# Transposing by DMA in place of TensorE, and alternating weight-gradient passes with dx tiles

## The chip, the cores and the metric

The kernel runs on one core of a Trainium2 chip. The metric is the device time of one execution in microseconds (us). Engines are named as in the profile: PE is TensorE (PEld its weight loads), DVE is VectorE, ACT is ScalarE, POOL is GpSimd, SP is SyncE, which here only issues DMAs (transfers between memories that the DMA engines carry out). A queue name with a q (SPq, ACTq) is the sequencer that issues. To evict is to copy a finished result of PE out of its result memory (PSUM) by ACT or DVE. The granted clock is the share of full speed at which the profile shows PE running.

Executions of one kernel mostly agree within about 1%. The granted TensorE clock differs a little from run to run (0.92 to 0.97 in the runs below), and the time goes with it. A run more than 1.5% above the fastest of its kernel is told slow. Medians below are over all runs, ratios over the fast ones, and a difference under about 8 us is not explained from single traces.

## The reference, cut to what matters

The reference computes an output and, by `vjp`, seven results in all: the output, dx, and the gradients of five weights. S = 2048 tokens, D = 512, F = 1792, 32 heads of 16.

```python
def _fwd_reference(A_x, A_wqkv, A_wo, B_x, B_w_gate, B_w_up, B_w_down):
    xn = _layernorm(A_x)
    s = linear_attention(xn @ A_wqkv) @ A_wo      # phi(q), phi(k), v; kv and z summed over tokens
    g = _silu((_sigmoid(xn @ B_w_gate) * (xn @ B_w_up)) @ B_w_down)
    return A_x + s * g

def reference(...):
    _out, _vjp = jax.vjp(_f, A_x, A_wqkv, A_wo, B_w_gate, B_w_up, B_w_down)
    return (_out, *_vjp(grad_out))
```

What matters: the gradient of a weight sums over the tokens, and this kernel's matmuls sum over the partitions of their operands, so both operands need the tokens on the partitions. Stage 2 produces the gradients dg, du and the activation hh with features on the partitions. Somebody has to transpose 3 x 1792 x 2048 values, 22 MB in bf16.

Of the kernel before, what the change touches and what calls it, by code (L numbers as in the profile page):

```python
# [27 lines left out]
def kernel(  # L28
# [28 lines left out]
    xn_d = dram.tile([NST, P, D], bf16, name="xn_d")  # L57
    xnT_d = dram.tile([NST, P, KT * P], bf16, name="xnT_d")
    pq_d = dram.tile([NST, P, D], bf16, name="pq_d")
    pqT_d = dram.tile([NST, P, KT * P], bf16, name="pqT_d")  # L60
    pkT_d = dram.tile([NST, P, KT * P], bf16, name="pkT_d")
    vT_d = dram.tile([NST, P, KT * P], bf16, name="vT_d")
# [6 lines left out]
    hhT_d = dram.tile([NST, P, FT * P], bf16, name="hhT_d")  # L69
    dgT_d = dram.tile([NST, P, FT * P], bf16, name="dgT_d")  # L70
    duT_d = dram.tile([NST, P, FT * P], bf16, name="duT_d")
# [42 lines left out]

    with ExitStack() as p1ctx:
# [3 lines left out]
        nc.sync.dma_start(out=xall[:, 0:2, :], in_=x2[0:256, :].rearrange("(t p) d -> p t d", p=P))  # L119
        nc.sync.dma_start(out=Wqkv_sb, in_=A_wqkv.rearrange("(kt p) n -> p kt n", p=P))  # L120
        nc.sync.dma_start(out=xall[:, 2:NST, :], in_=x2[256:S, :].rearrange("(t p) d -> p t d", p=P))
# [6 lines left out]
        sp1 = p1ctx.enter_context(tc.tile_pool(name="sp1", bufs=5))  # L128
# [18 lines left out]
        def do_wt_jobs(n):  # L147
            for _ in range(n):
                if not wt_jobs:
                    return  # L150
                dst, blocks = wt_jobs.pop(0)
                nb = len(blocks)
                pW = ps1.tile([P, 8, P], bf16, name="pW", tag="wt", bufs=1)
                for k, blk in enumerate(blocks):
                    nc.tensor.transpose(pW[:, k, :], blk, ident)
                if wt_flip[0] % 2 == 0:
                    nc.vector.tensor_copy(out=dst, in_=pW[:, :nb, :].rearrange("p a b -> p (a b)"))
                else:
                    nc.scalar.activation(out=dst, in_=pW[:, :nb, :].rearrange("p a b -> p (a b)"), func=ACT.Identity)
                wt_flip[0] += 1  # L160

        for st in range(NST):
            if st >= 2:
                do_wt_jobs(2)
            x_t = xall[:, st, :]
            stats = p1.tile([P, nc.vector.BN_STATS_DIM], f32, name="stats")
            nc.vector.bn_stats(out=stats, in_=x_t)
            mv = p1.tile([P, nc.vector.BN_AGGR_DIM], f32, name="mv")
            nc.vector.bn_aggr(out=mv, in_=stats)
            vpe = p1.tile([P, 1], f32, name="vpe")  # L170
            nc.vector.tensor_scalar(out=vpe, in0=mv[:, 1:2], scalar1=EPS_LN, scalar2=None, op0=ALU.add)
            nc.gpsimd.tensor_tensor(out=rstd_all[:, st:st + 1], in0=vpe, in1=neghalf, op=ALU.pow)
            xn_t = xn_all[:, st, :]
            nc.vector.tensor_scalar(out=xn_t, in0=x_t, scalar1=mv[:, 0:1], scalar2=rstd_all[:, st:st + 1],
                                    op0=ALU.subtract, op1=ALU.mult)
            pT = ps1.tile([P, KT, P], bf16, name="pT", tag="tr", bufs=2)
            for kt in range(KT):
                nc.tensor.transpose(pT[:, kt, :], xn_t[:, kt * P:(kt + 1) * P], ident)
            xnT_t = sp1.tile([P, KT, P], bf16, name="xnT_t")
            nc.vector.tensor_copy(out=xnT_t, in_=pT)  # L180
            nc.sync.dma_start(out=xnT_d[st], in_=xnT_t.rearrange("p a b -> p (a b)"))
            qkv_ps = []
            for w in range(3):
                pm = ps1.tile([P, D], f32, name="pm", tag="mm", bufs=3)
                for kt in range(KT):
                    nc.tensor.matmul(pm, lhsT=xnT_t[:, kt, :], rhs=Wqkv_sb[:, kt, w * D:(w + 1) * D],  # L186
                                     start=(kt == 0), stop=(kt == KT - 1))
                qkv_ps.append(pm)
            phis = []
            for w in range(2):  # L190
                e1 = p1.tile([P, D], bf16, name="e1")
                nc.scalar.activation(out=e1, in_=qkv_ps[w], func=ACT.Exp)
                bb = p1.tile([P, D], bf16, name="bb")
                nc.vector.tensor_scalar(out=bb, in0=e1, scalar1=1.0, scalar2=EPS_PHI, op0=ALU.min, op1=ALU.add)
                ph = sp1.tile([P, D], bf16, name=f"ph{w}")
                nc.vector.scalar_tensor_tensor(out=ph, in0=qkv_ps[w], scalar=1.0 + EPS_PHI, in1=bb,
                                               op0=ALU.add, op1=ALU.max)
                phis.append(ph)
            pq_t, pk_t = phis
            v_t = p1.tile([P, D], bf16, name="v_t")  # L200
            nc.scalar.activation(out=v_t, in_=qkv_ps[2], func=ACT.Identity)
            nc.sync.dma_start(out=pq_d[st], in_=pq_t)
            for src, dst, nm in ((pq_t, pqT_d, "pqT"), (pk_t, pkT_d, "pkT"), (v_t, vT_d, "vT")):
                pT2 = ps1.tile([P, KT, P], bf16, name="pT2", tag="tr", bufs=2)
                for j in range(KT):
                    nc.tensor.transpose(pT2[:, j, :], src[:, j * P:(j + 1) * P], ident)
                tT = sp1.tile([P, KT, P], bf16, name="tT_" + nm)
                nc.scalar.activation(out=tT, in_=pT2, func=ACT.Identity)
                nc.sync.dma_start(out=dst[st], in_=tT.rearrange("p a b -> p (a b)"))
            for j in range(KT):  # L210
                nc.tensor.matmul(kv_ps[:, j, :], lhsT=pk_t[:, j * P:(j + 1) * P], rhs=v_t[:, j * P:(j + 1) * P],
                                 start=(st == 0 and j == 0), stop=(st == NST - 1 and j == KT - 1),
                                 skip_group_check=True)
            for j in range(KT):
                nc.tensor.matmul(z_ps[:, j:j + 1], lhsT=pk_t[:, j * P:(j + 1) * P], rhs=ones_col,
                                 start=(st == 0 and j == 0), stop=(st == NST - 1 and j == KT - 1),
                                 skip_group_check=True)
# [5 lines left out]
        pT3 = ps1.tile([P, KT, P], bf16, name="pT3", tag="tr", bufs=2)  # L223
        for j in range(KT):
            nc.tensor.transpose(pT3[:, j, :], KVm_sb[:, j, :], ident)
        nc.vector.tensor_copy(out=KVmT_sb, in_=pT3)
        for j in range(KT):
            nc.vector.tensor_scalar(out=Zc_sb[:, j, :], in0=hsel, scalar1=zacc[:, j:j + 1], scalar2=None, op0=ALU.mult)
        zct_ps = ps1.tile([P, KT, P], f32, name="zct_ps", tag="mm", bufs=3)
# [6 lines left out]
    with ExitStack() as p2ctx:  # L236
# [11 lines left out]
        state = {}  # L248

        def fwd(st):  # L250
# [3 lines left out]
            xnT_t = ld.tile([P, KT, P], bf16, name="xnT_t")  # L254
            nc.sync.dma_start(out=xnT_t.rearrange("p a b -> p (a b)"), in_=xnT_d[st])
            pqT_t = ld.tile([P, KT, P], bf16, name="pqT_t")
            nc.sync.dma_start(out=pqT_t.rearrange("p a b -> p (a b)"), in_=pqT_d[st])
            pq_t = ld.tile([P, D], bf16, name="pq_t", bufs=2)
            nc.sync.dma_start(out=pq_t, in_=pq_d[st])
# [64 lines left out]
            nc.gpsimd.dma_start(out=hhT_d[st], in_=hhT_c.rearrange("p a b -> p (a b)"))  # L324
            s.update(sgT_c=sgT_c, nsgT_c=nsgT_c, hhT_c=hhT_c, b_ps=b_ps)

        def bwd(st):
# [123 lines left out]
            nc.gpsimd.dma_start(out=dgT_d[st], in_=dgT_c.rearrange("p a b -> p (a b)"))  # L451
            nc.gpsimd.dma_start(out=duT_d[st], in_=duT_c.rearrange("p a b -> p (a b)"))
# [9 lines left out]
    with ExitStack() as p3ctx:  # L462
        big = p3ctx.enter_context(tc.tile_pool(name="big3", bufs=1))
        ld3 = p3ctx.enter_context(tc.tile_pool(name="ld3", bufs=2))
        tp3 = p3ctx.enter_context(tc.tile_pool(name="tp3", bufs=2))
        dwl = p3ctx.enter_context(tc.tile_pool(name="dwl", bufs=3))
        psw3 = p3ctx.enter_context(tc.tile_pool(name="psw3", bufs=4, space=PSUM))
        psdw = p3ctx.enter_context(tc.tile_pool(name="psdw", bufs=4, space=PSUM))

        Wqkv_sb3 = big.tile([P, KT, 3 * D], bf16, name="Wqkv_sb3")  # L470
        nc.sync.dma_start(out=Wqkv_sb3, in_=A_wqkv.rearrange("(kt p) n -> p kt n", p=P))
        WqkvT_sb = big.tile([P, 3 * KT, D], bf16, name="WqkvT_sb")
        db_all = big.tile([P, NST, D], bf16, name="db_all")
        o_all = big.tile([P, NST, D], bf16, name="o_all")
        dso_all = big.tile([P, NST, D], bf16, name="dso_all")
        dq_all = big.tile([P, NST, D], bf16, name="dq_all")
        dk_all = big.tile([P, NST, D], bf16, name="dk_all")
        dv_all = big.tile([P, NST, D], bf16, name="dv_all")

# [31 lines left out]
        for j0 in range(0, 3 * KT, 2):  # L511
            pW3 = psw3.tile([P, 8, P], bf16, name="pW3", tag="w")
            for jj in range(2):
                for kt in range(KT):
                    nc.tensor.transpose(pW3[:, jj * KT + kt, :], Wqkv_sb3[:, kt, (j0 + jj) * P:(j0 + jj + 1) * P], ident)
# [152 lines left out]
```

## The kernel before: the parts that the change touches

There are 16 token tiles of 128 (NST), 4 blocks of D (KT), 14 blocks of F (FT). Three stages follow each other, with scratch tensors in DRAM between them.

Stage 1 transposes four things per tile on PE (16 transposes), evicts them and stores them:

```python
for st in range(NST):
    ...                                             # layernorm on DVE -> xn_t
    for kt in range(KT):
        nc.tensor.transpose(pT[:, kt, :], xn_t[:, kt * P:(kt + 1) * P], ident)
    nc.vector.tensor_copy(out=xnT_t, in_=pT)
    nc.sync.dma_start(out=xnT_d[st], in_=xnT_t.rearrange("p a b -> p (a b)"))
    ...                                             # QKV matmuls, phi, v
    for src, dst, nm in ((pq_t, pqT_d, "pqT"), (pk_t, pkT_d, "pkT"), (v_t, vT_d, "vT")):
        for j in range(KT):
            nc.tensor.transpose(pT2[:, j, :], src[:, j * P:(j + 1) * P], ident)
        nc.scalar.activation(out=tT, in_=pT2, func=ACT.Identity)
        nc.sync.dma_start(out=dst[st], in_=tT.rearrange("p a b -> p (a b)"))
    ...                                             # kv and z sums
```

Stage 2 does forward and backward of each tile and stores hhT, dgT and duT as whole tiles (one 3584-byte row per partition). Stage 3 first runs 16 dx tiles, then twelve passes that load, transpose and use those tensors, then four plain passes:

```python
for st in range(NST):                               # the dx tiles ("tile loop")
    ... # loads pkT, vT, dqT, dO, dxnp; dkT_t on DVE; dvT_t, dk_all, dv_all on ACT; 12 matmuls into dxn_ps

def load_T(src_d, st, f0, f1):
    nc.sync.dma_start(out=lt[:, :n, :]..., in_=src_d[st][:, f0 * P:f1 * P])
    for k in range(n):
        nc.tensor.transpose(pT6[:, k, :], lt[:, k, :], ident)
    evac(tok[:, :n * P], pT6[:, :n, :]...)          # ACT and DVE in turn
    return tok

for src_d, out_w in ((dgT_d, out_4), (duT_d, out_5)):
    for (f0, f1) in FGROUPS:                        # (0,4) (4,8) (8,12) (12,14)
        accs = [...] * KT
        for st in range(NST):
            tok = load_T(src_d, st, f0, f1)
            for a in range(KT):
                nc.tensor.matmul(accs[a][:, :n * P], lhsT=xn_all[:, st, a * P:(a + 1) * P], rhs=tok[:, :n * P], ...)
        finish(accs, ...)
...                                                 # the same for hhT_d against db_all
simple_pass(o_all, dso_all, ...)                    # four passes of 64 matmuls without transposes
simple_pass(xn_all, dq_all, ...); simple_pass(xn_all, dk_all, ...); simple_pass(xn_all, dv_all, ...)
```

## Time and profile before

The median was 955.19 us in three runs. The profiled execution spans 957.1 us.

| Stretch of the profile before | us | what limits it |
|---|---|---|
| 0-34 first loads | 34 | DMA: 289 GB/s; PE busy 7 us |
| 34-123 stage 1, 16 tiles | 89 | PE 76, ACT 63 busy |
| 140-524 stage 2, most of it | 384 | PE 348 |
| 556-580 start of stage 3 | 24 | DMA and the transposes of Wqkv |
| 580-679 16 dx tiles | 99 | waits; PE 68 |
| 679-897 twelve passes with transposes | 218 | PE 200 |
| 897-950 plain passes | 53 | PE 52 |

The lines behind the table are from the view by stretches, kernel before. After the two ends and the length stand the busy time of each engine and, in brackets, its instructions; the last three columns are the granted clock, the mean busy share of the 16 DMA engines, and GB/s.

```profile
core 0: us, PE busy (x) PEld busy (x) DVE busy (x) ACT busy (x) POOL busy (x), PEclk, DMA share, GB/s
34.00:123.00 89.00, 76.28 (x721) 47.51 (x735) 49.97 (x117) 62.58 (x104) 4.32 (x8) 0.98 0.35 113
140.00:524.00 384.00, 348.06 (x3724) 246.96 (x3780) 212.64 (x418) 158.15 (x292) 198.13 (x246) 0.96 0.34 116
556.00:580.00 24.00, 6.54 (x55) 5.05 (x53) 4.05 (x13) 3.67 (x4) 1.54 (x3) 0.64 0.95 327
580.00:679.00 99.00, 68.16 (x517) 40.09 (x524) 53.87 (x137) 37.31 (x63) 24.51 (x29) 0.92 0.60 185
679.00:897.00 218.00, 200.28 (x1399) 112.27 (x1422) 53.84 (x126) 62.46 (x120) 26.43 (x49) 1.00 0.42 125
```

See two kinds of stretch. In the passes PE is full and the DMA engines are at 0.42, so PE work that can move to DMA is time. In the tile loop PE has 31 us of holes. The waits of PE in that loop name the holes (what waited, what released it, us in total, times, longest):

```profile
PE pT L553 <- DVE dkT_t L545: 27.2, 13, 7.0
```

### The profile page before, as it was taken

The page shows a single profiled execution, that of the slowest core. Times are in us where ns is not written, and L with a number is a line of the kernel's source. Part 1 is how long each engine was busy: PE and PEld are TensorE (multiplying, and loading weights), DVE is VectorE, ACT ScalarE, POOL GpSimd, SP SyncE. Part 2 cuts the span into 40 slices and gives each one's busy share as a digit, 9 for nine tenths or more (in the row PEclk, how much of TensorE's full clock was granted, in tenths as well). Part 3 has the DMA queues.
Part 4 walks back from the last instruction along what each step waited for, and adds up shares of the span by engine and source line. Part 5 has one row for each costly group of instructions (what it writes and reads, how often), then busy time and mean ns, then how long its engine had stood idle before and what let it go on. Part 6 is the DMA issues. An engine that isn't in the chain of part 4 may idle for free. (4 is left out here: it accounts for less than half of the span.)

```text
span 957.1 us, 18060 instructions
## 1 busy us (share of the span) xinstructions
PE 798.9 (83%) x7044; PEld 505.9 (53%) x7160; DVE 418.9 (44%) x925; ACT 348.9 (36%) x625; POOL 291.4 (30%) x397
## 2 busy tenths in 40 slices
PE   2489888889998889888999754677898899899996
PEld 1355466666666666666666432344444555554443
DVE  1955446555445565555544621566422222222101
ACT  1377654344444433444444221344323223223100
POOL 1300026454545554555454510223201101101111
PEclk9799989999999999999999976999999999999999
DMA  9333343333233332333322278755343444444111
GB/s 321 145 116 117 123 124 102 124 121 130 103 123 113 130 124 91 115 127 117 130 92 106 79 254 259 218 171 170 111 127 116 138 134 124 130 132 129 49 39 45
DMA packets 90471, 124.94 MB, mean 131 GB/s; under 512 B 10961, under 2 KB 76753, under 8 KB 90385
## 3 DMA queue, kind: packets, MB, share of 16 engines
q1 hardware_dynamic: 65344, 60.85, 21.2%
q0 software_dynamic: 13344, 48.51, 14.0%
q10 hardware_dynamic: 11696, 14.42, 4.5%
q8 instruction: 56, 0.92, 0.4%
q14 instruction: 31, 0.25, 0.1%
HBM read 64.75 MB, written 58.98 MB: 129 GB/s over the span
## 5 line engine op out<-in xcount | busy, mean ns | idle before, releaser
L621 PE MATMUL dwacc<-dw_tok,xn_all 128*128 128x512 bf16 (+1 forms) x496 | 105.9, 351 | 7.4 <-DVE dw_tok L508 2.7
L506 ACT ACTIVATE dw_tok<-pT 128x512 bf16<-128x512 bf16 (+1 forms) x96 | 50.5, 543 | 150.3 <-PE pT L609 129.0
L593 POOL DMA_DIRECT2D out_dram<-dwres x62 | 33.2, 539 | 236.1 <-ACT dwres L506 209.6
L508 DVE COPY dw_tok<-pT 128x512 bf16<-128x512 bf16 (+1 forms) x96 | 37.1, 391 | 134.8 <-PE pT L609 129.2
L427 PE MATMUL dxn_ps<-WuT_sb,duT_c 128*128 128x512 bf16 x224 | 88.5, 395 | 0.8
L434 POOL TENSOR_TENSOR btT<-hhT_c,nsgT_c 128x512 bf16<-128x512 bf16 x64 | 71.7, 1127 | 39.2 <-DVE dgT_c L446 20.0
L621 PEld LDWEIGHTS <-xn_all 128*128 128x128 bf16 x512 | 49.4, 97 | 50.3 <-issue 11.0
L425 PE MATMUL dxn_ps<-WgT_sb,dgT_c 128*128 128x512 bf16 x192 | 75.9, 395 | 0.0
L314 PE MATMUL u_ps<-xnT_t,Wu_sb 128*128 128x128 bf16 x896 | 73.5, 230 | 0.0
L321 DVE TENSOR_TENSOR hhT_c<-sgT_c,u_ps 128x512 bf16<-128x512 bf16 x64 | 39.7, 621 | 76.4 <-PE u_ps L314 76.4
L444 ACT ACTIVATE dh<-dh_ps 128x512 bf16<-128x512 f32 x64 | 34.8, 544 | 102.7 <-PE dh_ps L439 102.7
L439 PE MATMUL dh_ps<-dbT_t,WdT_sb 128*128 128x128 bf16 x896 | 71.0, 224 | 1.3 <-ACT dh L444 0.7
L439 PEld LDWEIGHTS <-WdT_sb 128*128 128x128 bf16 x896 | 58.8, 100 | 13.4 <-issue 2.1
L308 PE MATMUL g_ps<-xnT_t,Wg_sb 128*128 128x128 bf16 x896 | 64.2, 222 | 0.0
L609 PE MATMUL pT<-ident,dw_lt 128*128 128x128 bf16 x672 | 55.2, 219 | 8.0 <-DMA dw_lt<-dgT_d 4.5
L308 PEld LDWEIGHTS <-Wg_sb 128*128 128x128 bf16 x896 | 55.9, 99 | 7.8
L609 PEld LDWEIGHTS <-dw_lt 128*128 128x128 bf16 x672 | 44.4, 98 | 28.7 <-DMA dw_lt<-dgT_d 6.3
L314 PEld LDWEIGHTS <-Wu_sb 128*128 128x128 bf16 x896 | 59.3, 104 | 0.2
L508 DVE CAST dwres<-dwacc 128x512 bf16<-128x512 f32 (+1 forms) x31 | 20.4, 657 | 78.9 <-PE dwacc L599 42.2
L630 PE MATMUL dwacc<-db_all,dw_tok 128*128 128x512 bf16 x216 | 52.9, 380 | 2.3 <-ACT dw_tok L506 0.8
L186 PE MATMUL pm<-Wqkv_sb,xnT_t 128*128 128x512 bf16 x179 | 43.8, 396 | 10.1 <-DVE xnT_t L180 6.8
L319 ACT ACTIVATE sgT_c<-g_ps 128x512 bf16<-128x512 f32 x64 | 34.8, 544 | 44.5 <-PE g_ps L308 39.3
(199 smaller groups left out, 1429.4 us busy)
## 6 DMA issues: line engine op xcount, KB each, us to landing
hhT_d<-hhT_c POOLq DMA_DIRECT2D x16, 448.0 KB, 2.8
duT_d<-duT_c POOLq DMA_DIRECT2D x16, 448.0 KB, 2.8
dgT_d<-dgT_c POOLq DMA_DIRECT2D x16, 448.0 KB, 4.2
out_dram<-dwres POOLq DMA_DIRECT2D x54, 128.0 KB, 2.1
dw_lt<-dgT_d SPq DMA_DIRECT2D x48, 128.0 KB, 2.2
dw_lt<-duT_d SPq DMA_DIRECT2D x48, 128.0 KB, 2.3
dw_lt<-hhT_d SPq DMA_DIRECT2D x48, 128.0 KB, 2.2
dO_t<-in_grad_out_dram SPq DMA_DIRECT2D x32, 128.0 KB, 2.0
```

The costliest lines, as they stand in the source:

```text
L186: nc.tensor.matmul(pm, lhsT=xnT_t[:, kt, :], rhs=Wqkv_sb[:, kt, w * D:(w + 1) * D], start=(kt == 0), stop=(kt == KT - 1))
L308: nc.tensor.matmul(g_ps[:, fi, :], lhsT=Wg_sb[:, kt, ft * P:(ft + 1) * P], rhs=xnT_t[:, kt, :], start=(kt == 0), stop=(kt == KT - 1))
L314: nc.tensor.matmul(u_ps[:, fi, :], lhsT=Wu_sb[:, kt, ft * P:(ft + 1) * P], rhs=xnT_t[:, kt, :], start=(kt == 0), stop=(kt == KT - 1))
L425: nc.tensor.matmul(dxn_ps, lhsT=dgT_c[:, ft, :], rhs=WgT_sb[:, ft, :], start=(cnt[0] == 0), stop=False)
L427: nc.tensor.matmul(dxn_ps, lhsT=duT_c[:, ft, :], rhs=WuT_sb[:, ft, :], start=False, stop=(cnt[0] == 2 * FT - 1))
L434: nc.gpsimd.tensor_tensor(out=btT[:, :n, :], in0=hhT_c[:, f0:f1, :], in1=nsgT_c[:, f0:f1, :], op=ALU.mult)
L439: nc.tensor.matmul(dh_ps[:, fi, :], lhsT=WdT_sb[:, dt, ft * P:(ft + 1) * P], rhs=dbT_t[:, dt, :], start=(dt == 0), stop=(dt == KT - 1))
L506: nc.scalar.activation(out=dst, in_=src, func=ACT.Identity)
L508: nc.vector.tensor_copy(out=dst, in_=src)
L609: nc.tensor.transpose(pT6[:, k, :], lt[:, k, :], ident)
L621: nc.tensor.matmul(accs[a][:, :n * P], lhsT=xn_all[:, st, a * P:(a + 1) * P], rhs=tok[:, :n * P], start=(st == 0), stop=(st == NST - 1))
L630: nc.tensor.matmul(accs[k], lhsT=tok[:, k * P:(k + 1) * P], rhs=db_all[:, st, :], start=(st == 0), stop=(st == NST - 1))
```

## The change

Its intent: take the transposes of large operands off PE by letting the DMA transpose while it loads (some expectations below call what does this the crossbar); and trace the weight-gradient passes between groups of four dx tiles, so that pass matmuls can fill PE while a tile waits.

```diff
-    xnT_d / pqT_d / pkT_d / vT_d: transposed copies, one per tile
+    pq_d = dram.tile([S, D]); pk_d = dram.tile([S, D]); v_d = dram.tile([S, D])   # plain
-    hhT_d = dram.tile([NST, P, FT * P], bf16)       # and dgT_d, duT_d
+    hhT_d = dram.tile([F, S], bf16)                 # and dgT_d, duT_d
...  stage 1, by groups of four tiles
+    nc.gpsimd.tensor_scalar(out=xn_all[:, st, :], in0=x_t, scalar1=rstd_all[:, st:st + 1], scalar2=nmr, ...)
+    nc.sync.dma_start_transpose(out=xnT_g, in_=xn_all[:, 4 * g:4 * g + 4, :].rearrange("p t d -> p (t d)"))
-    16 PE transposes and 4 evictions per tile
...  stage 2: xnT and pqT come as transposed groups; the stores become rows of 256 bytes
-    nc.gpsimd.dma_start(out=hhT_d[st], in_=hhT_c.rearrange("p a b -> p (a b)"))
+    nc.gpsimd.dma_start(out=hhT_dv[:, :, tsl], in_=hhT_c)
...  stage 3
+    def load_tokT(src_d, f0, f1, name):             # one operand of a pass, 2 MB
+        nc.sync.dma_start_transpose(out=t[:, :, :n * P], in_=src_d[f0 * P:f1 * P, :])
+    first_tok = load_tokT(dgT_d, 0, 4, "tok")
+    nc.sync.dma_start_transpose(out=WqkvT_sb, in_=A_wqkv)
-    dqT_t, dO_t, dxnp_t issued by nc.sync
+    dqT_t, dO_t, dxnp_t issued by nc.scalar
+    def pass_xn_lhs(rhs_tok, n_cols, out_fn):       # one accumulator after the other, 5 PSUM buffers
+        for a in range(KT):
+            for st in range(NST): nc.tensor.matmul(acc[:, :n_cols], lhsT=xn_all[...], rhs=rhs_tok[:, st, :n_cols], ...)
+            finish_one(acc, n_cols, out_fn(a))
+    load_pkv_group(0)
+    for g in range(NG):
+        if g + 1 < NG: load_pkv_group(g + 1)        # pkT_g, vT_g by DMA transpose
+        for sl in range(4): phase3_tile(4 * g + sl, *pk_groups[g])
+        for _ in range(3): passes[pi](); pi += 1
```

All DMA transposes are issued by SP.

## The prediction

> **What bounds the kernel now.** The stretches view splits the 957 us profile into three stages. Stage 1 (0-135 us: layernorm, QKV, weight transposes): the load phase runs to 34 us with PE busy only 7 us; then 89 us for 16 tiles, PE busy 76, ACT 63, DVE 50. Stage 2 (135-558, forward and backward tiles): PE busy 369 of 410 us, its only large wait 29 us for dnum; PE-bound. Stage 3 (558-957): 22 us of start, bounded by transfers and Wqkv transposes; a tile loop 580-679, PE busy 68 of 99, waiting 27 us on dkT_t; twelve weight-gradient passes with PE transposes 679-897; four plain passes to 950. The DMA share is only 0.3-0.6 in most of it.
>
> **What the change removes.** 976 of 7160 matmul-type instructions (instruction order of both programs): 672 transposes of dg/du/hh, 256 in stage 1, 48 of Wqkv.
> - Passes: a plain pass takes 13.7 us for 64 matmuls (214 ns each), a full pass with 64 transposes about 19.6. So 5.9 us x 9, and about 6 x 3 for the shorter ones: about -70 us, all on the critical path because PE is full there.
> - Tile loop: four to seven pass matmuls now sit in each tile's dkT_t wait, and the single-tile pk/v loads, which the chain of waits shows holding PE, become prefetched groups: about -22 us.
> - Stage 1: 16 transposes per tile leave PE (about 1.4 us per tile), three 0.59 us evictions leave ACT, and one 0.42 us copy leaves DVE; normalising goes to POOL, which is nearly idle. Estimate 89 to 62 us; the load phase stays. About -27 us.
>
> **What it adds.**
> - About 33 MB of DMA transposes, all on one queue: each 2 MB operand must land within a 13.7 us pass. Stage 3 needs 26 MB in about 270 us, so break-even is about 100 GB/s. The Trainium skill, "DMA: Bandwidth & Descriptors", Latency and other measured facts, gives 261 GB/s effective for a DMA transpose. Estimate from it: 8 us per 2 MB, hidden. No run of mine shows it yet; this is the largest risk.
> - 48 stores of hhT/dgT/duT in rows of 256 B: 1792 runs in place of 128, with descriptors written by POOL. Today such an issue costs 0.54-0.58 us. POOL is busy about 13 us of each 26 us tile, so it can take about 4 us more per store. I estimate 1-4 us each, mostly hidden: +10 us in stage 2 for btT coming later.
> - Exposed transposes at the start of stages 1, 2 and 3: about +5 us.
>
> **Sum.** 955 - 70 - 22 - 27 + 10 + 5 = 851; with a little for the risks, **858 us**. Range 810 to 1010. Faster by over 2%: 0.72; within 2%: 0.08; slower: 0.20.
>
> **What would show each step.** Passes: the dwacc matmuls have no pT waits, and 64 take about 14 us. Transposes: the landing time of a 2 MB tok in the DMA view, 8-12 us, and no PE wait on tok. POOL: DMA issue of hhT_d/dgT_d/duT_d below 4 us; stage 2 still about 425-435 us with PE about 90% busy. Stage 1: its end moves from 135 to about 105 us. Stage 3: about 400 to 305 us.
>
> **What would make it wrong.** Transposes below 100 GB/s: stage 3 then becomes a stream of transfers with PE waiting on tok, pkT_g and vT_g, 26 MB at 60 GB/s being 430 us, and the kernel is slower. Descriptor writing at over 6 us per store: POOL then bounds stage 2, which grows by up to 100 us and eats the gain. Transposes from SBUF could be far slower than from DRAM and delay each group of four tiles in stage 1.

## More of the kernel before

Part of a full pass, seen in order of time (start, length, engine, line, what, count). PE alternates transposes (L609) and matmuls (L630):

```profile
847.25 2.76 PE L630 MATMUL dwacc<-db_all,dw_tok 128*128 128x512 bf16 x12
849.85 1.20 PE L609 MATMUL pT<-ident,dw_lt 128*128 128x128 bf16 x15
850.98 2.76 PE L630 MATMUL dwacc<-db_all,dw_tok 128*128 128x512 bf16 x12
853.58 0.78 PE L609 MATMUL pT<-ident,dw_lt 128*128 128x128 bf16 x11
854.61 2.54 PE L630 MATMUL dwacc<-db_all,dw_tok 128*128 128x512 bf16 x11 [0.26 <-DVE dw_tok L508]
856.99 0.89 PE L609 MATMUL pT<-ident,dw_lt 128*128 128x128 bf16 x13
857.95 2.76 PE L630 MATMUL dwacc<-db_all,dw_tok 128*128 128x512 bf16 x12
```

From 847.25 to 857.95 lie 35 matmuls and 39 transposes in 10.70 us. Pass matmuls without transposes run at 219 ns, as a piece of the changed kernel's chain of waits shows (start, length, what, count):

```profile
607.50 10.74 PE dwacc L603 x49
```

So 39 transposes took 10.70 - 35 x 0.219 = 3.0 us, 78 ns each. At that rate 672 of them are an estimated 52 us.

## The result, and the profile after

The changed kernel took 849.37 us (median of 12 runs, 841.07 to 851.48) against 957.7 us for the kernel before (15 runs, 953.23 to 960.74). A ratio here and below is the mean time of one kernel's fast runs over the mean time of the other's fast runs of the same rounds, so it is not quite the ratio of the medians. It is 0.8852, 95% interval 0.8826 to 0.8879: 11.5% faster. The prediction was 858 us, with 0.72 for faster.

The view by stretches, changed kernel, same columns as above: stage 1's tiles, most of stage 2, the start of stage 3, and then tiles and twelve passes together.

```profile
31.00:97.00 66.00, 60.35 (x484) 33.51 (x491) 40.74 (x99) 42.35 (x64) 35.35 (x62) 1.00 0.42 116
116.00:502.00 386.00, 350.21 (x3726) 249.46 (x3784) 214.16 (x418) 158.16 (x292) 221.68 (x246) 0.96 0.44 112
538.00:575.00 37.00, 4.18 (x12) 1.39 (x12) 1.47 (x8) 0.00 (x0) 1.67 (x3) 0.54 1.14 185
575.00:787.00 212.00, 205.26 (x1219) 107.02 (x1243) 63.76 (x164) 50.02 (x87) 51.56 (x77) 0.99 0.92 216
```

In place of 317 us for tiles and passes (580-897), with PE busy 268, there are now 212, with PE busy 205 of them. The price is on the third line: 37 us in which PE did 4 us of work. (A DMA share over 1, as there, is printed as the view gives it.) Cutting both profiled runs at the same events on PE gives the whole account. (The events are the last b_ps matmul of the first and of the last tile, the last matmul of stage 2, the first dpkT_ps matmul of stage 3, and the last pass matmul.)

| Stretch between events | before | after | change |
|---|---|---|---|
| stage 1 and first tile's forward | 139.9 | 116.2 | -23.7 |
| stage 2, 15 tiles | 384.5 | 386.0 | +1.5 |
| stage 2, rest | 32.5 | 34.4 | +1.9 |
| end of stage 2 to first dx tile | 24.7 | 38.4 | +13.7 |
| dx tiles and all passes | 367.8 | 266.8 | -101.0 |
| end | 7.7 | 5.5 | -2.2 |
| sum | 957.1 | 847.3 | -109.8 |

The longest waits of PE in the changed kernel:

```profile
PE tr_ps L399 <- DVE dnum L385: 29.8, 16, 2.4
PE dwacc L603 <- DMA tok<-dgT_d: 29.7, 1, 29.7
PE pm L192 <- DMA xnT_g<-xn_all: 21.0, 1, 21.0
```

The first is stage 2's old wait. The second is new: eight pass matmuls of the first operand stand ahead of the first dx tile in PE's order, and that 2 MB operand lands late. The source issues it first, but in the trace the 1.5 MB transpose of Wqkv goes ahead of it and holds SP for 12.9 us (start, length of the issue):

```profile
536.64 12.93 SPq L497 DMA_TRANSPOSE WqkvT_sb<-in_A_wqkv_dram  x1
551.16 16.41 SPq L493 DMA_TRANSPOSE tok<-dgT_d  x1
```

The third is stage 1's start, which was a load phase before as well.

The transposed transfers, from the list of DMA issues (KB are not given for transposes; the last number is the median us from issue to landing), with the store in 256-byte rows last. Before, a store of hhT landed in 2.8 us:

```profile
tok<-dgT_d SPq DMA_TRANSPOSE x4, 17.2
tok<-duT_d SPq DMA_TRANSPOSE x4, 13.9
tok<-hhT_d SPq DMA_TRANSPOSE x4, 11.7
hhT_d<-hhT_c POOLq DMA_DIRECT2D x16, 448.0 KB, 4.8
```

These are medians of four, of which one is 1 MB; the 2 MB operands alone took 10.6 to 19.2 us, and not the 8 us of the estimate. But a pass lasts 14 us and operands are loaded up to four ahead (five buffers), so after the first one PE has no wait on them in the list.

### The profile page after: what moved, and what is told of

Same layout as the page of the kernel before. It is cut to its first block, busy times and chain, and to the rows that moved or that the text cites. A ratio compares the mean times of both kernels' runs of the same rounds, so it can differ in the third digit from the quotient of the medians.

```text
span 847.3 us, 15187 instructions
## 1 busy us (share of the span) xinstructions
PE 719.6 (85%) x6083; PEld 446.7 (53%) x6184; DVE 365.6 (43%) x806; ACT 274.0 (32%) x482; POOL 356.0 (42%) x461
## 5 line engine op out<-in xcount | busy, mean ns | idle before, releaser
L603 PE MATMUL dwacc<-tok,xn_all 128*128 128x512 bf16 (+1 forms) x503 | 101.8, 356 | 30.1 <-DMA tok<-dgT_d 29.7
L603 PEld LDWEIGHTS <-xn_all 128*128 128x128 bf16 x704 | 68.6, 98 | 97.5 <-issue 31.6
L327 PE MATMUL u_ps<-xnT_g,Wu_sb 128*128 128x128 bf16 x896 | 73.9, 231 | 0.0
L452 PEld LDWEIGHTS <-WdT_sb 128*128 128x128 bf16 x896 | 61.1, 103 | 13.6 <-issue 2.5
L321 PE MATMUL g_ps<-xnT_g,Wg_sb 128*128 128x128 bf16 x896 | 64.9, 222 | 1.6 <-DVE ZcT_sb L235 1.6
L192 PE MATMUL pm<-Wqkv_sb,xnT_g 128*128 128x512 bf16 x184 | 44.8, 391 | 21.4 <-DMA xnT_g<-xn_all 21.0
L525 ACT ACTIVATE dwres<-dwacc 128x512 bf16<-128x512 f32 (+1 forms) x31 | 17.5, 569 | 136.5 <-PE dwacc L603 76.8
L591 POOL TENSOR_TENSOR dx_t<-tt,dO_t 128x512 bf16<-128x512 f32 x16 | 18.4, 1151 | 96.5 <-DVE tt L589 96.5
L611 PE MATMUL dwacc<-db_all,tok 128*128 128x512 bf16 x218 | 49.3, 379 | 0.3
L330 PE MATMUL b_ps<-Wd_sb,hhT_c 128*128 128x512 bf16 x162 | 45.1, 379 | 1.6
L458 DVE TENSOR_TENSOR duT_c<-dh,sgT_c 128x512 bf16<-128x512 bf16 x64 | 28.6, 446 | 31.0 <-ACT dh L457 30.9
```

The lines of the kernel that those rows point to most:

```text
L192: nc.tensor.matmul(pm, lhsT=xnT_g[:, sl * KT + kt, :], rhs=Wqkv_sb[:, kt, w * D:(w + 1) * D], start=(kt == 0), stop=(kt == KT - 1))
L321: nc.tensor.matmul(g_ps[:, fi, :], lhsT=Wg_sb[:, kt, ft * P:(ft + 1) * P], rhs=xnT_t[:, kt, :], start=(kt == 0), stop=(kt == KT - 1))
L327: nc.tensor.matmul(u_ps[:, fi, :], lhsT=Wu_sb[:, kt, ft * P:(ft + 1) * P], rhs=xnT_t[:, kt, :], start=(kt == 0), stop=(kt == KT - 1))
L330: nc.tensor.matmul(b_ps, lhsT=hhT_c[:, ft, :], rhs=Wd_sb[:, ft, :], start=(ft == 0), stop=(ft == FT - 1))
L452: nc.tensor.matmul(dh_ps[:, fi, :], lhsT=WdT_sb[:, dt, ft * P:(ft + 1) * P], rhs=dbT_t[:, dt, :], start=(dt == 0), stop=(dt == KT - 1))
L603: nc.tensor.matmul(acc[:, :n_cols], lhsT=xn_all[:, st, a * P:(a + 1) * P], rhs=rhs_tok[:, st, :n_cols], start=(st == 0), stop=(st == NST - 1))
```

## The experiments

All runs gave correct results except e3, which is wrong on purpose. Each was timed in three rounds beside the kernel before, except where it is said. Two theories stood from the start. Theory T: the gain is the transposes taken off PE, with a smaller part from the overlap. Theory O: the gain is the overlap and the new order of the accumulators, and PE transposes had been nearly hidden.

### a0_after: the yardstick

No edit.

> The changed kernel itself, unaltered, as the yardstick for the three runs beside it. Every theory: about 849 us, ratio to the kernel before 0.88 to 0.89.

Measured: 845.60 us (843.09 to 849.11), ratio 0.8844 (0.8810 to 0.8878).

### e1_tiles_first and e1b_no_overlap: what is the alternation worth?

```diff
             for sl in range(4):
                 phase3_tile(4 * g + sl, *pk_groups[g])
-            for _ in range(3):
-                if pi < len(passes): passes[pi](); pi += 1
```

e1b has the same edit, and pins the first matmul of every accumulator of the twelve passes (and of one plain pass) behind everything traced before it on PE:

```diff
+                    if st == 0:
+                        tc.keep_in_program_order(mm)
```

> The changed kernel with all 16 dx tiles traced first and the weight-gradient passes after them, so that the source no longer alternates groups of tiles and passes; the scheduler may still put pass matmuls of the first pass into the tiles' waits. Theory A (the alternation itself is worth little: what helps is that a few pass matmuls fill each tile's wait, which still happens): within 8 us of the changed kernel, 841 to 857. Theory B (the alternation is worth its 20 us, because it spreads the pk/v and operand transposes over the stage): 865 or more.

> As e1, but every pass accumulator is pinned behind all tiles in PE's order, so no pass matmul fills a tile's wait. The DMA transposes stay. If the fill is worth what the prediction gave it (22 us), the tile loop goes back to about 5.2 us per tile and the time is about 865 to 875, less up to 15 us because the tiles no longer stand behind the first 2 MB operand. Theory A, the fill is worth about 1 us per tile and the start hole is given back: 845 to 865. If interleaving is the main gain (a rival to the transposes): 890 or more.

Measured: e1 878.91 us, ratio 0.9208 (0.9160 to 0.9256); e1b 879.31 us, ratio 0.9206 (0.9152 to 0.9259). Both are 33 us over the yardstick beside them. e1 kept four or five pass matmuls in each tile's wait and was no faster than e1b, which had none. So theory A of these two runs fell, while 879 us lies in none of e1b's three ranges. With the tiles together the fill gains nothing on the whole; the alternation of groups and passes is worth 33 us. The fill does its own work: PE's waits on dkT_t are gone in e1. But its waits on dvT_t have grown in their place (e1 first, then e1b's two; the profiles are of e1's slowest and e1b's fastest run; in the changed kernel 5.1 us on dvT_t and none listed on dkT_t):

```profile
PE dxn_ps L570 <- ACT dvT_t L555: 30.6, 4, 9.3
```

```profile
PE dxn_ps L570 <- ACT dvT_t L555: 14.4, 4, 6.1
PE pT L558 <- DVE dkT_t L550: 11.2, 16, 0.7
```

e1b also gives the terms of the sum apart, because its tiles and passes do not mix. The view by stretches, e1b, tiles and then the twelve passes:

```profile
571.00:668.00 97.00, 70.66 (x504) 39.65 (x513) 47.22 (x135) 36.32 (x63) 24.09 (x29) 0.89 0.89 202
668.00:813.00 145.00, 144.32 (x724) 71.98 (x736) 16.55 (x29) 13.69 (x24) 27.45 (x49) 1.00 0.69 179
```

The tile loop takes 97 us, as long as in the kernel before (99), although its pk and v loads are now prefetched groups. The passes take 145 us where they took 218. So the transposes and the waits around them were worth about 73 us, and the overlap has to hide the rest of the tile loop's holes. The passes also have a new order of accumulators, but that cannot be the 73 us: the plain pass of dv, which has no transposes in either kernel, took 13.7 us with four accumulators at once before and 13.6 with one after the other in the changed kernel (first to last start in both traces). While the tiles run, the DMA engines are at 0.89.

### e2_pe_tok: the transposes back on PE

The operands are loaded plain, and each pass transposes its operand on PE per token tile, with four accumulators at once as before. All else in the source stays, the alternation included.

```diff
-            nc.sync.dma_start_transpose(out=t[:, :, :n * P], in_=src_d[f0 * P:f1 * P, :])
+            for a in range(n): nc.sync.dma_start(out=t[:, a * nb:(a + 1) * nb, :n * P], in_=...)   # plain
+        def pe_tok(raw, st, n):
+            for k in range(n): nc.tensor.transpose(pT6[:, k, :], raw[...], ident)
+            evac(tok[:, :n * P], pT6[:, :n, :].rearrange("p a b -> p (a b)"))
```

> The operands of the twelve transposing passes are loaded plain and transposed on PE again (672 transposes, evictions on ACT and DVE, four accumulators at once as in the kernel before); all else as in the changed kernel, the alternation of tiles and passes included. If the transposes on PE cost about 71 us in the passes, as predicted, and the start of the stage gets some 15 us shorter for lack of a 2 MB transpose: 895 to 925. Rival (the gain came from the accumulator order and the overlap, PE transposes hide behind matmuls): 870 or less.

Measured: 964.19 us, ratio 1.0086 (1.0050 to 1.0122). This is far from theory O (870 or less was its mark), but my own 895 to 925 was missed as well. The run lost the whole gain and more. The waits of PE, e2, and then the wait of DVE in its passes, show where the surplus is:

```profile
PE dwacc L634 <- DVE dw_tok L530: 17.8, 8, 4.7
PE dwacc L644 <- DVE dw_tok L530: 9.1, 6, 4.4
PE dwacc L634 <- ACT dw_tok L528: 7.4, 23, 1.1
```

```profile
DVE dwres L530 <- DMA out_dram<-dwres: 60.6, 11, 7.1
```

At the end of a pass four result evictions stand in DVE's and ACT's order ahead of the next operand's evictions, and they wait for a result buffer whose store has not landed. PE then waits for dw_tok. In the passes of the kernel before, DVE's wait of this kind was 15.3 us. PE's waits on dkT_t in the tiles were also back, 18.9 us in this trace, so part of the overlap was lost too. So e2 is not a clean reversal: it says that having the transposes back on PE costs more than the prediction gave them, but not how much of that is the transposes themselves. The cleaner number, which refutes theory O, is e1b against the kernel before: 145 against 218 us, without any overlap.

### e3_plain_tok: are the DMA transposes hidden?

```diff
-            nc.sync.dma_start_transpose(out=t[:, :, :n * P], in_=src_d[f0 * P:f1 * P, :])
+            for a in range(n): nc.sync.dma_start(out=t[:, a * nb:(a + 1) * nb, :n * P], in_=...)   # same bytes, not transposed
```

> Wrong result on purpose: each transposed 2 MB operand of the passes is replaced by a plain load of the same bytes, without transposing; dW of gate, up and down come out wrong. Theory A (the DMA transposes are hidden behind the passes except for the first one, before which PE sits idle 30 us): only the start gets shorter, 825 to 842, and PE is as busy as before in the middle of stage 3. Theory B (stage 3 is now bound by the transposes, whose rate is near the 100 GB/s break-even): 815 or less. It also shows what a plain load of 2 MB takes beside the 12 to 17 us of the transposed one; if the crossbar cost nothing, they would be equal.

Measured: 831.98 us, ratio 0.8682 (0.8647 to 0.8718), three weight gradients wrong as intended. That is theory A's range. The wait on the first operand fell from 29.7 to 16.8 us. In what is left of it the plain load stands on SP behind the transpose of Wqkv (issued at 537.1 us, 13.7 us long) and waits 1.6 us more for the last store of dgT. So of the cost of transposing the pass operands by DMA about 15 us is exposed (by the ratios of e3 and a0_after), 13 of it in that one wait.

### e4_pkv_first: the start of stage 3 in another order

```diff
-        first_tok = load_tokT(dgT_d, 0, 4, "tok")
         nc.sync.dma_start_transpose(out=WqkvT_sb, in_=A_wqkv)
+        load_pkv_group(0)
+        first_tok = load_tokT(dgT_d, 0, 4, "tok")
...      in the first pass only
+                    if pin and st == 0: tc.keep_in_program_order(mm)
```

> Start of stage 3 reordered: the weight transpose and the first pk/v group are issued before the first 2 MB operand, and the first pass is pinned behind the first four tiles on PE. Theory A (PE's 38 us hole at the start of stage 3 is the order of one transfer queue: four tiles of about 5 us fit while the first operand lands): 15 to 22 us less than the changed kernel, 827 to 836. Theory B (the hole is the total of transfers that must land before PE can work, so moving one ahead delays the next as much): within 6 us of the changed kernel.

Measured: 838.83 us (833.02 to 843.44), ratio 0.8760 (0.8712 to 0.8808). In its trace, as in the changed kernel's, SP issues the transpose of Wqkv first, so what really moved is the pk/v group and the first pass. The first dx tile starts 25.6 us after stage 2's last matmul and not 38.4. But the four tiles that now run while the operand lands take 20 us without pass matmuls beside them, so part of the gain is given back. The result lies between the two theories: about 7 us under the yardstick by the medians, 1% by the ratios.

### e5_double_stores: do the 256-byte stores cost anything?

```diff
             nc.gpsimd.dma_start(out=hhT_dv[:, :, tsl], in_=hhT_c)
+            nc.gpsimd.dma_start(out=hhT_x[:, :, tsl], in_=hhT_c)      # and dg, du; never read
```

> Each of the 48 stores in rows of 256 bytes is made a second time, to scratch tensors that nobody reads. POOL gets 3.3 us more per tile of about 25.7, and 1.3 MB more per tile to write. Theory A (these stores are hidden with room to spare): less than 6 us more than the changed kernel, stage 2 within 1%. Theory B (they already delay stage 2 or the DMA engines are near full there): 20 us more or worse.

Measured: 846.73 us, ratio 0.8858 (0.8808 to 0.8909): no difference from the changed kernel. Doubling the suspected cost moved nothing, so it is hidden with room to spare. The stretch of stage 2, e5:

```profile
116.80:493.80 377.00, 337.75 (x3728) 238.40 (x3786) 217.84 (x418) 158.11 (x292) 265.32 (x289) 1.00 0.72 166
```

POOL was busy 265 of 377 us. That the stage was even 9 us shorter than in the changed kernel's trace goes with its granted clock (1.00 against 0.96), not with the stores: a warning against reading single traces to better than that.

### e6_xnT_pe_all: stage 1's xn on PE again

```diff
-            nc.sync.dma_start_transpose(out=xnT_g, in_=xn_all[:, 4 * g:4 * g + 4, :]...)
+            for h in range(2):
+                for k in range(8): nc.tensor.transpose(pX[:, k, :], xn_all[...], ident)
+                nc.vector.tensor_copy(out=xnT_g[:, 8 * h:8 * h + 8, :], in_=pX)
```

> In stage 1 xn is transposed on PE again for all four groups (64 transposes, 8 evictions of 1024 columns on DVE), in place of four DMA transposes; pq, pk and v stay on DMA. Theory A (the first DMA transpose waits behind 3 MB of loads on its queue and holds PE 21 us): PE starts about 15 us earlier, pays 6 us for its own transposes: stage 1 ends 4 to 12 us earlier, 837 to 846. Theory B (stage 1 cannot start before the x and weight loads have landed at 31 us whatever transposes xn): 849 to 858.

Measured: 851.30 us, ratio 0.8895 (0.8867 to 0.8923), theory B's range. The first QKV matmul came at 15 us and not at 31, yet PE stood still again:

```profile
PE pW L157 <- DVE WoT_sb L159: 15.3, 1, 15.3
```

In DVE's order the layernorm statistics of the later tiles, whose x lands only at 22 us, stand before the eviction that PE needs. The start of stage 1 is held by the loads through more than one chain, and putting the transposes of xn back on PE gained nothing.

### e9_loads_off_act: why does the alternation matter?

In e1 the trace put 26.8 us of ACT's waits down to a transposed operand, `tok<-duT_d`. ACT itself does not use that operand. But it issues the three small loads of each dx tile, and in e1's chain of waits ACT issued such a load at 637.90 us, just after a `tok<-duT_d` of 18.3 us that began at 619.48, with dvT_t behind it. That suggested theory L. The edit to e1:

```diff
-            nc.scalar.dma_start(out=dqT_t..., in_=dqT_d[st])          # and dO_t, dxnp_t
+            nc.gpsimd.dma_start(out=dqT_t..., in_=dqT_d[st])
```

> As e1_tiles_first (879 us, tiles traced first), but the three small loads of each dx tile (dqT, dO, dxnp) are issued by POOL and no longer by ACT. Theory L (in e1, ACT stands still because its next small load must wait for a completion semaphore that a 2 MB transposed operand still holds, and the evictions behind it in ACT's order wait too; that is what the alternation hid): the waits of PE on dvT_t fall from 31 us to under 10, time 845 to 862. Theory M (with the tiles first, the tiles are slow because the transposes fill the DMA engines, whoever issues the small loads): 870 or more.

Measured: the four runs took 868.5 to 885.5 us, median 879.11; two were told slow, and the ratio of the fast ones (875.78 and 868.5) is 0.9105 (0.9056 to 0.9155). The profile is of one of the slow runs, so it is read here for where the waits went and not for small differences. PE's wait on dvT_t vanished from its list, but PE now waited as long for dkT_t, the tile's other chain:

```profile
PE pT L558 <- DVE dkT_t L550: 33.1, 6, 12.5
```

The small loads themselves took long (list of DMA issues, e9):

```profile
dqT_t<-dqT_d POOLq DMA_DIRECT2D x16, 128.0 KB, 9.3
dxnp_t<-dxnp_d POOLq DMA_DIRECT2D x16, 256.0 KB, 10.8
```

In the kernel before they landed in 2.3 and 2.9 us. By the fast runs e9 is about 1% faster than e1 (0.9105 against 0.9208), on another chip. So theory L falls as the main cause of the 33 us, though it may hold a part, about 10 us by these ratios. Theory M's range (870 or more) is met only just: the two fast runs have a mean of 872.1. For theory M speaks that in e9's chain of waits small transfers of 10.7 to 12.6 us stand between PE's pieces. But it is not shown. If slow small loads made the 33 us, they would be slow in both e1 and e1b and fast in the changed kernel. They are not (list of DMA issues; the changed kernel, e1, e1b):

```profile
dqT_t<-dqT_d ACTq DMA_DIRECT2D x16, 128.0 KB, 5.9
```

```profile
dqT_t<-dqT_d ACTq DMA_DIRECT2D x16, 128.0 KB, 7.0
```

```profile
dqT_t<-dqT_d ACTq DMA_DIRECT2D x16, 128.0 KB, 3.0
```

What remains of theory M is that the alternation gives the loads time: the blocks of pass matmuls between the groups of four tiles last 31 to 36 us in the changed kernel. That is argued and not shown; why the tiles wait more when they stand together stays open. The Trainium skill, "DMA: Bandwidth & Descriptors", section Issuing engines are not separate DMA queues, says that DMAs of all issuers run on the same 16 engines and that another issuer saves only sequencer time. This run agrees in the main: another issuer took about 1% off e1's time, and about 25 us of distance to the changed kernel stayed (0.9105 against 0.8844). The skill also says, in "Perfetto Trace Analysis", Optimization Strategy, that where the most-contended engine changes over time, interleaving the regimes may improve performance. The 33 us between e1b and the yardstick are such a case: in e1b's view above the DMA engines are at 0.89 with PE busy 71 of 97 us in the tiles, and at 0.69 with PE busy 144 of 145 us in the passes.

### e10_start_and_loads: e4 with the small loads on POOL

> As e4_pkv_first (839 us) with the same three small loads issued by POOL. Theory L gives a little, since in the alternating order PE waits on dvT_t only 3 us: 828 to 839, at best. If POOL, which also issues the stores of results, is held up by them instead: 845 or more. A candidate for a version better than both kernels.

Measured: 847.09 us, ratio 0.8831 (0.8805 to 0.8856), so worse than e4; one of the four runs, 869.62 us, was told slow. ACT waited 49.8 us for result buffers whose stores had not landed (15.6 in e4). POOL issues those stores, and in its order they now stand among loads that wait for buffers, which is the likely reason.

### e11_rate_alone: the disputed cost by itself

One look, no rounds. After a barrier at the end of the changed kernel, six transfers run one after the other:

```diff
+        tc.strict_bb_all_engine_barrier()
+        for rep in range(2):
+            nc.sync.dma_start_transpose(out=rate_t, in_=dgT_d[0:512, :])                   # 2 MB, DRAM
+            nc.sync.dma_start(out=rate_t..., in_=dgT_d[0:512, :]...)                       # 2 MB, plain
+            nc.sync.dma_start_transpose(out=rate_t[:, :, 0:128], in_=xn_all[:, 0:4, :]...) # 0.5 MB, SBUF
```

> The changed kernel with six transfers after a barrier at its end, one after the other, with nothing else running: 2 MB transposed from DRAM, the same 2 MB plain, 0.5 MB transposed from SBUF, twice. The outputs stay right; about 30 to 60 us longer. If the crossbar runs at the rate that I took for the prediction, 2 MB land in about 8 us; if the 12 to 17 us of the passes are its own rate and not contention, in 12 or more. Plain: 6 to 8 us.

Measured (list of DMA issues of that stretch, us from issue to landing last):

```profile
rate_t<-dgT_d SPq DMA_DIRECT2D x2, 2048.0 KB, 7.8
rate_t<-dgT_d SPq DMA_TRANSPOSE x2, 9.5
rate_t<-xn_all SPq DMA_TRANSPOSE x2, 4.3
```

Alone, 2 MB land transposed in 9.5 us (2.10 MB / 9.5 us = 221 GB/s), plain in 7.8. So the 12 to 17 us inside stage 3 are contention and not the transposing transfer's own rate. (Two transfers of each kind, one run.) The same trace shows what SP pays, in order of time (start, length of the issue):

```profile
845.55 7.41 SPq L695 DMA_TRANSPOSE rate_t<-dgT_d  x1
855.04 0.39 SPq L696 DMA_DIRECT2D rate_t<-dgT_d  x1
862.90 1.32 SPq L698 DMA_TRANSPOSE rate_t<-xn_all  x1
```

Issuing the transpose occupies SP for 7.4 us, the plain load for 0.4 us.

### e13_best: e4 with the gate and up weights loaded later

```diff
-        nc.scalar.dma_start(out=Wg_sb, ...); nc.scalar.dma_start(out=Wu_sb, ...)
...      in the first tile of stage 1, behind its evictions on ACT
+                    tc.keep_in_program_order(nc.scalar.dma_start(out=W_t, in_=...))
```

> e4_pkv_first (839 us) with one more edit: the loads of the gate and up weights (3.7 MB of the 9.8 MB that fill the first 31 us) are issued from ACT only after the first tile's evictions. Theory A (stage 1 starts when the bytes queued ahead of its first operands have landed, so fewer bytes there start it earlier): the first QKV matmul comes at 20 to 25 us instead of 31, and stage 1 ends 5 to 9 us earlier: 829 to 835 us, a version better than both kernels. Theory B (the start waits for the chain of layernorm on DVE and POOL, or the postponed loads collide with stage 1's stores and transposes): 837 us or more.

Measured in five rounds: 848.23 us (842.29 to 850.83), ratio 0.8854 (0.8828 to 0.8880). Theory A got its first half: the first QKV matmul came at 24.5 us. But stage 1 did not end earlier (the first tile's last b_ps matmul at 118.1 us against 115.0 in e4), with a new wait of PE on DVE's ph of 10.8 us. The label was a hope. Why the whole run is 9 us over e4 is not settled: stage 1 explains 3 us of it, and in the profiles PE also waited 9.8 us for dvT_t in stage 3, against 3.0 in e4.

So the best version found is e4_pkv_first at 838.83 us. It beats the kernel before (ratio 0.8760) and, by about 1%, the changed kernel (0.8844 in a0_after); the intervals, 0.8712 to 0.8808 and 0.8810 to 0.8878, just fail to touch, and the two were measured on different chips.

## Why the prediction was right, point by point

| Term of the prediction | predicted | measured | by |
|---|---|---|---|
| passes without PE transposes | -70 | -73 | 218 before, 145 in e1b |
| overlap of tiles and passes | -22 | -33 | a0_after against e1b |
| stage 1 | -27 | -24 | events, both traces |
| 256-byte stores in stage 2 | +10 | +2 | events; e5 |
| exposed transposes | +5 | +14 | end of stage 2 to first dx tile, both traces |
| total | 858 us with 7 us for risks | 849 us | 12 runs |

The measured terms come from different pairs of runs and add up to -114 us, where the medians differ by 108. That the sum came within 9 us of the result is partly luck: the overlap and the stores turned out 11 and 8 us better than predicted, the start of stage 3 about 9 us and stage 1 3 us worse.

- **What bounded the kernel.** Right: PE in the passes, and waits in the tile loop. Removing PE work from the passes was worth its full time. By the estimate above, the 73 us are about 52 us of transposes at 78 ns each; the rest would be the waits around them. Without any overlap (e1b) the change is still worth 78 us.
- **"about -22 us" for the tile loop.** The direction was right and the size too small. The prediction credited "four to seven pass matmuls" in each tile's wait, and the prefetched pk/v groups. e1 and e1b show that with the tiles together the fill gains nothing on the whole, because the waits on dvT_t grow (30.6 us against 14.4), and that the tile loop stays at about 97 us with the prefetched groups. The term is made by the blocks of pass matmuls between groups of tiles. Why the tiles wait less then is not settled (e9). The mechanism had been named wrongly although the sum came out.
- **"each 2 MB operand must land within a 13.7 us pass", 8 us estimated.** The estimate from the 261 GB/s of the Trainium skill ("DMA: Bandwidth & Descriptors", Latency and other measured facts) was close to the transfer alone (9.5 us in e11) and too low inside the kernel (12 to 17 us). The break-even argument held: the operands arrive ahead of PE, except the first.
- **"Exposed transposes ... about +5 us".** Mis-sized: 13.7 us at the start of stage 3 alone. I had not seen in the instruction order that eight pass matmuls stand ahead of the first dx tile on PE, and that their operand is queued ahead of the tile's own and behind the transpose of Wqkv. Of the 29.7 us of wait, e3 takes 13 back; e4 starts the first tile 13 us earlier but gains only about 7.
- **"I estimate 1-4 us each, mostly hidden: +10 us".** An issue took 1.10 to 1.15 us, at the low end, and stage 2 did not notice, nor did it notice twice as many (e5).
- **"Stage 1: its end moves from 135 to about 105 us".** The corresponding point moved from 139.9 to 116.2. The tiles' stretch became 66 us against 62 predicted.

## What to carry to other kernels

Where PE was full and the DMA engines were not (0.42 here), transposes moved into loads were worth PE's time for them. Check first that the bytes over the stretch leave a margin, and look at what the first transfer makes PE wait for, since it has nothing to hide behind. Here, with the DMA engines near full (0.9), it was worth 33 us to put blocks of work with landed operands between the pieces that need fresh ones, while moving the small loads to another issuing engine gained about 1% in one place (e9) and lost 1% in another (e10). Costing a change term by term and measuring the terms apart finds the ones that were right for the wrong reason.

## What the Trainium skill lacked or had wrong

- "Advanced Engine Details and Errata", X-Bar Transpose (TRN2), says that transpose DMAs are as fast as regular ones, at 350-400 GB/s. Alone, 2 MB from DRAM landed in 9.5 us transposed and 7.8 us plain (e11): 221 against 269 GB/s, counted from issue to landing, so with the start and end of the transfer in it.
- The effective rate of 261 GB/s in "DMA: Bandwidth & Descriptors", Latency and other measured facts, lies near the transfer alone (221 in e11), but among other traffic a 2 MB operand took 10.6 to 19.2 us (109 to 198 GB/s). The page gives no figure for a transpose in company.
- No page that I read gives, for this chip, the time that a 2 MB transpose from DRAM holds its issuing queue: 7.4 us alone and 16.4 us for the first operand in the changed kernel, against 0.39 us for a plain load. What stood next on that queue was issued behind it (the first pk group at 567.8 us, after the operand's 551.2 + 16.4).
- No page that I read gives what many short rows cost the POOL queue: 1792 rows of 256 bytes took 1.10 to 1.15 us per issue where 128 long rows took 0.54 to 0.58, so about 0.3 ns per added row (0.56 us / 1664), an estimate, and landed in 4.8 us in place of 2.8 (hhT).
